# V sums of an attention kernel in four one-bank PSUM tiles, and the last batch's turns split between VectorE and TensorE

## The chip, the cores and the metric

The kernel runs on one NeuronCore of a Trainium2 chip. The metric is the device time of one execution in microseconds. Before the change the median of three runs is 398.49 us (398.30 to 399.39).

## The reference

Two stages follow each other: an attention whose weights are sigmoids, and a soft mixture of experts over all 3584 rows of its output.

```python
# q, k, v: (8 batches, 12 heads, 448 rows, 64)
scores = (q @ k.T) / sqrt(64) - log(448)
attn = 1 / (1 + exp(-scores))
x = heads_side_by_side(attn @ v)          # (8*448, 768)
logits = x @ phi                          # (3584, 32 slots)
d = softmax(logits, axis=0)               # over all rows
slot_input = d.T @ x                      # (32, 768), 4 slots for each of 8 experts
slot_out[e] = relu(slot_input[e] @ w1[e]) @ w2[e]      # 768 -> 1024 -> 768
c = softmax(logits, axis=1)               # over the slots
out = c @ slot_out
```

All of it is float32. The softmax over all rows needs the last batch, so the experts can only start when the attention is over.

## The kernel before

**Attention.** Two heads are a pair; there are 6 pairs in a batch and 48 in all (`NP`). The 448 keys of a pair are three full chunks of 128 (c = 0, 1, 2) and a rest of 64; the rests of an even pair p and of pair p + 1 share one chunk (c = 3). Two pairs thus make seven units: (p,0) (p,1) (p,2) (p,3) (p+1,0) (p+1,1) (p+1,2). There are 21 units in a batch. The loop at L376 takes one unit in each step i: `score` of unit i (four matmuls with 64x64 weights, L146, into an `sc` tile of two PSUM banks, then one sigmoid on ScalarE, L150, into `att`), and `weigh` of unit i - 2 (four matmuls, L175, that add V products into `av`). There are two `sc` tiles.

**The V sums.** `av0` (even pairs) and `av1` (odd pairs) are PSUM tiles of two banks, `[P, 2, 512]`. A chunk's first 64 keys are summed in bank 0 and its last 64 in bank 1 (index t), since the two halves use different rows of the array. After c = 2, `evac_a` (ScalarE, L178) copies bank 1 to `x`; `evac_b` (VectorE, L182) adds bank 0 to it. For an even pair, the unit of the rests stands between the two: its matmuls (called the vl matmuls below, after their operand) add pair p's rest into bank 0 of `av0`, and then write pair p + 1's rest as the first product into bank 1 of `av1`. So `evac_a(p)` reads bank 1 of `av0` while the vl matmuls write bank 0 of the same tile.

```python
o, w = avs[p + t], vls[p // 2][row, r]
start, stop = t == 1, t == 0
nc.tensor.matmul(o[r, t, 0:S], w, att[row, h, :], start=start, stop=stop)
```

**Order.** The engines TensorE, ScalarE, VectorE and the load queue run their instructions in the order in which the code is written. The pool tracks a tile as a whole: a writer waits for the tile's earlier readers. ScalarE's order around a rest is: sigmoid of the unit before, `evac_a`, sigmoid of the rest's own step.

**Between units.** `x` is also needed turned, with rows on the partitions (`y`). VectorE turns it in 32x32 blocks (`turns`, L197); these small instructions wait in the list `todo` and are let out in every step by `work`. Once per batch there are the logits (L215, 24 matmuls), a softmax over them (`softmax_a` on VectorE, `softmax_b` on ScalarE, `softmax_c` on VectorE) and the slot sums (L270, 16 matmuls).

**The last batch.** The logits of its first five pairs (L394) stand behind the scores of the last unit; they are added in `lgt`, an `sc` tile of which VectorE first sets a corner (L390). Pairs 0 to 2 and 3 are turned by VectorE (`turns(0, 0, 3)` and `turns(1, 0, 1)`), pairs 4 and 5 by TensorE transposes against an identity (`turn_pe`, L206) into the two halves of one tile `px`, from which ScalarE (L414, L415, L301) and VectorE (L308, L309) copy them. `warm` (L191) gives TensorE matmuls whose result nobody reads. `last_job` takes the maximum (L294, L296, L298, L303, L305), the exponential (L306), the slot sums (L270) and the turned slot inputs `sT` (L317).

**Experts.** Weights come in units of 384 KB into a ring of 56 + 11 tiles (`wa`, `wb`). The first 56 are loaded during the attention; the 11 `wb` tiles lie where the attention's buffers were and are loaded as these come free. Every further load waits for a ring tile that has been used up; the first of them stands behind the first half of expert 0 (L443). The PSUM pools of this stage (`ps_h` for `ph`, `ps_t` for `pt`, `ps_o` for `po`) take the attention's banks in the order of their lines (L432 to L434). The stage ends with the output's rows, stored through the same load queue.

Of the kernel before, what the change touches and what calls it, by code (L numbers as in the profile page):

```python
# [9 lines left out]
F32 = mybir.dt.float32  # L10
F32R = mybir.dt.float32r
AF = mybir.ActivationFunctionType
ALU = mybir.AluOpType
AX = mybir.AxisListType
PSUM = bass.MemoryType.PSUM

B, H, S, D = 8, 12, 448, 64
DM, NSLOT, E, SPE, F = 768, 32, 8, 4, 1024
P = 128
NFK = 3  # L20
# [14 lines left out]
WN = 128  # L35
CW = 256
NBK = 4
# [11 lines left out]
def soft_moe_attention(ctx: ExitStack, tc: tile.TileContext, qk, v, vl, phi, w1, w2, cst, out):  # L49
    nc = tc.nc  # L50
# [7 lines left out]
    ident = csb[:, 0:128]  # L58
# [6 lines left out]
    acc = small.tile([P, SLN], F32, name="acc")  # L65
# [31 lines left out]
    with ExitStack() as actx:  # L97
# [4 lines left out]
        ps_sc = actx.enter_context(tc.tile_pool(name="ps_sc", bufs=2, space=PSUM))  # L102
        ps_av = actx.enter_context(tc.tile_pool(name="ps_av", bufs=1, space=PSUM))
# [8 lines left out]
        def x_of(p):  # L112
            t, k = divmod(p % NPR, TR)
            return xs[t][:, k, :]
# [38 lines left out]
        def weigh(u):  # L153
            p, c = u
            att = atts.pop(u)
            if c == 0 and p % 2 == 0:
                avs[p] = ps_av.tile([P, 2, 512], F32, name="av0")
            if c == NFK:
                avs[p + 1] = ps_av.tile([P, 2, 512], F32, name="av1")
            if p == NP - 1:  # L160
                for h, r in enumerate(heads):
                    nc.tensor.matmul(
                        avs[p][r, 1, 0:S], vts[p][:, c, r], att[:, h, :], start=False, stop=(c == NFK - 1))
                return
            for t in range(2):
                row = slice(64 * t, 64 * t + 64)
                for h, r in enumerate(heads):
                    if c < NFK:
                        o, w = avs[p], vts[p][row, c, r]
                        start = c == 0 and (p % 2 == 0 or t == 0)  # L170
                        stop = c == NFK - 1 and (p % 2 == 1 or t == 1)
                    else:
                        o, w = avs[p + t], vls[p // 2][row, r]
                        start, stop = t == 1, t == 0
                    nc.tensor.matmul(o[r, t, 0:S], w, att[row, h, :], start=start, stop=stop)  # L175

        def evac_a(p):
            nc.scalar.copy(x_of(p), avs[p][:, 1, 0:S])  # L178

        def evac_b(p):  # L180
            av = avs.pop(p)
            nc.vector.tensor_tensor(out=x_of(p), in0=x_of(p), in1=av[:, 0, 0:S], op=ALU.add)  # L182

        def evac_last(p):
            x, av = x_of(p), avs.pop(p)
            for t in (slice(0, 2 * P), slice(2 * P, S)):
                nc.scalar.copy(x[:, t], av[:, 1, t])

        def warm(pw, n):
            for _ in range(n):  # L190
                nc.tensor.matmul(pw[:, 1, 0:P], ident, ident, start=True, stop=True)  # L191

        def turns(t, k0, n):
            def one(a, g):
# [8 lines left out]
        def turn_pe(px, p):  # L203
            for c in range(NBK):
                n = P if c < NBK - 1 else 64
                nc.tensor.transpose(out=px[0:n, c * P:(c + 1) * P], in_=x_of(p)[:, c * P:c * P + n], identity=ident)  # L206

        def y_of(px, p):
            y = ys[1][:, :, p % TR, :, :].rearrange("p a c k -> p c a k")
            return y, px.rearrange("p (c a k) -> p c a k", c=NBK, a=4)  # L210

        def logits(lg, b, pairs, js=(3, 2, 1, 0)):
            for hp in pairs:
# [71 lines left out]
        def last_job(b, lgt, pw, px):  # L285
            lg = lgt[:, 0, 0:P]
            pa = lgt[:, 1, :]
            old = mz[:, (b - 1) % 2:(b - 1) % 2 + 1]
            t1 = small.tile([P, 2, 132], F32, name="t1")
            pe, zt = t1[:, 0, 0:P], t1[:, 1, 0:P]  # L290
            m1 = small.tile([P, 8], F32, name="m1")
            cw = small.tile([P, 8], F32, name="cw")
            p = b * NPR + NPR - 1
            nc.vector.tensor_reduce(out=m1[:, 0:1], in_=lg, axis=AX.X, op=ALU.max)  # L294
            turn_pe(px[:, 1, :], p)
            nc.tensor.matmul(pa[0:1, 0:P], m1[:, 0:1], ident, start=True, stop=True)  # L296
            mrow = small.tile([1, 1, NSLOT], F32, name="mrow")
            nc.vector.tensor_reduce(  # L298
                out=mrow[:], in_=pa[0:1, 0:P].rearrange("o (j s) -> o s j", j=4), axis=AX.X, op=ALU.max)
            y, yx = y_of(px[:, 1, :], p)  # L300
            nc.scalar.copy(y[:, 0:2], yx[:, 0:2])  # L301
            for j in range(4):
                nc.tensor.matmul(pa[32 * j:32 * j + 32, P:P + 1], mrow[:, 0, :], csb[0:1, 0:1], start=True, stop=True)  # L303
            warm(pw, 2)
            nc.vector.tensor_scalar(cw[:, 0:1], pa[:, P:P + 1], old, -1.0, op0=ALU.max, op1=ALU.mult)  # L305
            nc.scalar.activation(pe, lg, AF.Exp, bias=cw[:, 0:1])  # L306
            nc.scalar.activation(cw[:, 1:2], old, AF.Exp, bias=cw[:, 0:1])
            nc.vector.tensor_copy(y[:, 2], yx[:, 2])  # L308
            nc.vector.tensor_copy(y[0:64, 3], yx[0:64, 3])  # L309
            nc.vector.transpose(zt, pe)  # L310
            warm(pw, 2)
            sl = ps_av.tile([P, 2, 512], F32, name="av1")[:, 0, :]
            slot_mm(sl, zt)
            nc.vector.scalar_tensor_tensor(
                out=acc[:], in0=acc[:], scalar=cw[:, 1:2], in1=sl[:, 0:SLN], op0=ALU.mult, op1=ALU.add)
            sT = small.tile([P, NKC, NSLOT], F32, name="phit")
            nc.vector.transpose(sT[:].rearrange("p k s -> p (k s)"), acc[:])  # L317
            nc.vector.transpose(lt_all[:, b, :], lg)  # L318
            nc.vector.tensor_reduce(out=cw[:, 4:5], in_=pe, axis=AX.X, op=ALU.add)
            nc.vector.scalar_tensor_tensor(  # L320
                out=cw[:, 6:7], in0=mz[:, 2:3], scalar=cw[:, 1:2], in1=cw[:, 4:5], op0=ALU.mult, op1=ALU.add)

            def finish(pool):
                pz = pool.tile([P, 512], F32, name="pt")
                nc.tensor.matmul(pz[:, 0:1], rep, cw[:, 6:7], start=True, stop=True)
                nc.vector.tensor_scalar(rz[:], pz[:, 0:1], 1e-9, None, op0=ALU.add)
                nc.vector.reciprocal(rz[:], rz[:])

            return sT, finish
# [6 lines left out]
        nc.sync.dma_start(phi_sb, phi)  # L336
        nc.sync.dma_start(csb[:], cst)
        load_qk(2)
        pw = ps_av.tile([P, 2, 512], F32, name="av0")
        for _ in range(WARM):  # L340
            nc.tensor.matmul(pw[:, 0, 0:WN], acc[:, 0:P], acc[:, 0:WN], start=True, stop=True)  # L341
        dmy = small.tile([1, 1], F32, name="dmy")
        nc.scalar.activation(dmy[:], nbias[0:1, :], AF.Sigmoid)

# [6 lines left out]
        for b in range(B):  # L351
            u = b * per_b + LAG
            late[u + 10] = [lambda: turns(0, 0, 3)]
            if b < B - 1:
                late[u + 17] = [lambda: turns(1, 0, 2)]
                late[u + 20] = [lambda: turns(1, 2, 1)]
            else:
                late[u + 13] = [lambda: turns(1, 0, 1)]
        for b in range(B - 1):
            u = (b + 1) * per_b + LAG  # L360
            early[u + 1] = [lambda b=b: logits_job(b)]
# [14 lines left out]
        for i in range(len(seq) + LAG):  # L376
# [20 lines left out]
            if i >= LAG:  # L397
                u = seq[i - LAG]
                weigh(u)
                p, c = u  # L400
                if c == NFK:
                    evac_b(p)
                    load_vl(p // 2 + 1)
                elif c == NFK - 1:
                    load_v(p + 2)
                    if p == NP - 1:
                        work(B * S)
                        pw = ps_av.tile([P, 2, 512], F32, name="av0")
                        px = ps_sc.tile([P, 2, 512], F32, name="sc")
                        turn_pe(px[:, 0, :], p - 1)  # L410
                        warm(pw, 2)
                        evac_last(p)
                        y, yx = y_of(px[:, 0, :], p - 1)
                        nc.scalar.copy(y[:, 0:3], yx[:, 0:3])  # L414
                        nc.scalar.copy(y[0:64, 3], yx[0:64, 3])  # L415
                        continue
                    evac_a(p)
                    if p % 2 == 1:
                        evac_b(p)
# [9 lines left out]
    for e in range(E):  # L429
        h = sb2.tile([P, 256], F32, name=f"h{e}", bufs=1)[:]  # L430
        hT.append(h.rearrange("p (f s) -> p f s", f=NFC))
    ps_h = ctx.enter_context(tc.tile_pool(name="ps_h", bufs=2, space=PSUM, reuse_waits="tile"))  # L432
    ps_t = ctx.enter_context(tc.tile_pool(name="ps_t", bufs=4, space=PSUM, reuse_waits="tile"))
    ps_o = ctx.enter_context(tc.tile_pool(name="ps_o", bufs=2, space=PSUM, reuse_waits="tile"))  # L434

    for _ in range(N_B):
# [181 lines left out]
```

## Time and profile before

The profiled execution took 397.56 us, of which 395.8 us are the span of the trace, so 1.76 us lie around it. It is 0.93 us under the median of the three runs.

| | value |
|---|---|
| time of the profiled execution, span | 397.56 us, 395.8 us |
| TensorE matmuls busy | 363.2 us (92%) |
| VectorE busy | 255.7 us (65%) |
| ScalarE busy | 223.2 us (56%) |
| moved by DMA | 95.26 MB, mean 241 GB/s |

The span has two parts: the attention up to about 302 us, in which TensorE is nearly always busy, and the experts with the output behind it, in which the DMA engines are. A share over the whole span tells little of either; each part is read by itself.

In the rows of the timeline the first two numbers are the start and the length in us; then come the engine (PE is TensorE's matmuls, DVE VectorE, ACT ScalarE, SPq the load queue), the line, the operation, what is written and read, and the count. In brackets is the time for which the engine sat idle before it and who ended that. A float32 matmul leaves two records here: four matmuls are "x8".

### The profile page before, as it was taken

The page shows a single profiled execution, that of the slowest core. Times are in us where ns is not written, and L with a number is a line of the kernel's source. Part 1 is how long each engine was busy: PE and PEld are TensorE (multiplying, and loading weights), DVE is VectorE, ACT ScalarE, POOL GpSimd, SP SyncE. Part 2 cuts the span into 40 slices and gives each one's busy share as a digit, 9 for nine tenths or more (in the row PEclk, how much of TensorE's full clock was granted, in tenths as well). Part 3 has the DMA queues.
Part 4 walks back from the last instruction along what each step waited for, and adds up shares of the span by engine and source line. Part 5 has one row for each costly group of instructions (what it writes and reads, how often), then busy time and mean ns, then how long its engine had stood idle before and what let it go on. Part 6 is the DMA issues. An engine that isn't in the chain of part 4 may idle for free.

```text
span 395.8 us, 10094 instructions
## 1 busy us (share of the span) xinstructions
PE 363.2 (92%) x4096; PEld 156.2 (39%) x4096; DVE 255.7 (65%) x688; ACT 223.2 (56%) x308; POOL 3.1 (1%) x14
## 2 busy tenths in 40 slices
PE   8999999999999999999999999999978988999750
PEld 5333444434343434434343444344345643422330
DVE  0158768786888688697868777886944782232450
ACT  5777667676766675675757666756731213422440
POOL 0000000000000000000000000000002000000000
PEclk9999999999999999999999999999989998999985
DMA  6677476656666675665676565433239999999998
GB/s 248 227 234 256 138 253 179 237 199 192 207 228 186 216 235 181 207 231 182 207 233 212 198 206 169 139 119 92 67 130 317 381 400 401 401 400 399 401 409 310
DMA packets 42382, 95.26 MB, mean 241 GB/s; under 512 B 4448, under 2 KB 18528, under 8 KB 42336
## 3 DMA queue, kind: packets, MB, share of 16 engines
q1 hardware_dynamic: 42336, 94.62, 69.0%
q8 instruction: 32, 0.52, 0.5%
q14 instruction: 14, 0.11, 0.1%
HBM read 83.59 MB, written 11.01 MB: 239 GB/s over the span
## 4 chain that ended last, share of the span: by engine, by line
PE 71%; DVE 10%; ACT 8%; DMA 5%; issue 2%; DVEq 0%; ACTq 0%; SPq 0%
PE sc L146 28%; PE av L175 28%; ACT att L150 4%; PE po L545 4%; PE sc L215 3%; DVE y L197 3%; PE sc L270 3%; DMA wa<-in_w_dram 2%; DMA wb<-in_w_dram 2%; ACT x L178 2%; PE pt L489 1%; DMA out_dram<-wa 1%; DVE tmp L458 1%; PE av L341 1%; DVE tmp L457 1%
## 5 line engine op out<-in xcount | busy, mean ns | idle before, releaser
L150 ACT ACTIVATE att<-sc,nbias 128x896 f32<-128x896 f32 x168 | 169.1, 1007 | 94.5 <-PE sc L146 91.8
L146 PE MATMUL sc<-qkt 64*64 64x448 f32 x1344 | 157.2, 538 | 0.4 <-ACT att L150 0.4
L197 DVE STREAM_TRANSPOSE y<-x 32x384 f32<-32x384 f32 (+5 forms) x368 | 148.0, 402 | 5.7
L175 PE MATMUL av<-att,v 64*64 64x448 f32 x1128 | 131.4, 536 | 0.0
L146 PEld LDWEIGHTS sc<-qkt 64*64 64x64 f32 x1344 | 49.8, 133 | 72.5 <-issue 66.1
L175 PEld LDWEIGHTS av<-att,v 64*64 64x64 f32 x1128 | 43.1, 133 | 62.8 <-issue 61.3
L182 DVE TENSOR_TENSOR x<-x,av 128x448 f32<-128x448 f32 x47 | 29.2, 621 | 49.6 <-PE av L175 40.2
L175 PE MATMUL av<-att,vl 64*64 64x448 f32 x192 | 23.2, 554 | 5.6 <-ACT x L178 4.5
L545 PE MATMUL po<-wa,h 128*32 128x384 f32 x224 | 25.6, 519 | 0.0
L178 ACT COPY x<-av 128x448 f32<-128x448 f32 x47 | 24.5, 522 | 0.0
L443 PE MATMUL ph<-wa,phit 128*32 128x256 f32 x336 | 18.5, 379 | 1.3 <-DVE lt_all L318 1.3
L509 DVE COPY wa<-pt 128x384 f32<-128x384 f32 x27 | 13.9, 553 | 8.4 <-PE pt L508 5.0
L509 ACT COPY wa<-ph 128x384 f32<-128x384 f32 x27 | 12.1, 479 | 11.1 <-PE ph L508 8.9
L215 PE MATMUL sc<-x,phit 128*32 128x96 f32 (+1 forms) x384 | 13.3, 274 | 2.2 <-DVE sc L390 2.2
L175 PEld LDWEIGHTS av<-att,vl 64*64 64x64 f32 x192 | 5.7, 132 | 21.9 <-ACT x L178 18.8
L443 PEld LDWEIGHTS ph<-wa,phit 128*32 128x32 f32 x336 | 10.8, 110 | 8.5 <-issue 1.7
L215 PEld LDWEIGHTS sc<-x,phit 128*32 128x32 f32 x384 | 10.7, 115 | 8.1 <-ACT x L178 4.9
L508 PE MATMUL ph<-st,wb 128*128 128x384 f32 x28 | 11.8, 422 | 1.1 <-DVE st L538 1.0
L281 DVE SCALAR_TENSOR_TENSOR acc<-acc,t,sc 128x192 f32<-128x192 f32 x6 | 2.5, 415 | 13.8 <-PE sc L270 13.8
L508 PE MATMUL pt<-st,wb 128*128 128x384 f32 x28 | 9.6, 341 | 1.6 <-DVE st L538 1.6
L460 ACT COPY h<-tmp 128x32 f32<-128x32 f32 x8 | 1.7, 218 | 16.2 <-DVE tmp L458 16.2
L270 PE MATMUL sc<-y,t 128*32 128x192 f32 x224 | 10.6, 329 | 0.0
(98 smaller groups left out, 159.2 us busy)
## 6 DMA issues: line engine op xcount, KB each, us to landing
wa<-in_w_dram SPq DMA_DIRECT2D x112, 384.0 KB, 5.0
qkt<-in_qk_dram SPq DMA_DIRECT2D x48, 448.0 KB, 3.5
out_dram<-wa SPq DMA_DIRECT2D x27, 384.0 KB, 5.6
v<-in_v_dram SPq DMA_DIRECT2D x48, 192.0 KB, 2.5
wb<-in_w_dram SPq DMA_DIRECT2D x16, 384.0 KB, 6.2
vl<-in_vl_dram SPq DMA_DIRECT2D x24, 64.0 KB, 1.9
out_dram<-wb SPq DMA_DIRECT2D x1, 384.0 KB, 7.6
csb<-in_cst_dram SPq DMA_DIRECT2D x1, 128.0 KB, 4.5
```

The lines of the kernel that those rows point to most:

```text
L146: nc.tensor.matmul(sc[64 * t:64 * t + 64, h, 0:S], qkts[pt][r, S + k0:S + k0 + 64], qkts[pt][r, 0:S], start=True, stop=True)
L150: nc.scalar.activation(att[:], sc[:, :, 0:S], AF.Sigmoid, bias=nbias[:], scale=QSCALE)
L175: nc.tensor.matmul(o[r, t, 0:S], w, att[row, h, :], start=start, stop=stop)
L178: nc.scalar.copy(x_of(p), avs[p][:, 1, 0:S])
L182: nc.vector.tensor_tensor(out=x_of(p), in0=x_of(p), in1=av[:, 0, 0:S], op=ALU.add)
L197: nc.vector.transpose(ys[t][32 * g:32 * g + 32, a, k0:k0 + n, 0:nblk(g), :], src)
L215: nc.tensor.matmul(lg[32 * j:32 * j + 32, 0:BLK * nblk(j)], phi_sb[:, hp, :], blocks(x_of(b * NPR + hp), j, nblk(j)), start=(hp == 0), sto ...
L270: nc.tensor.matmul(sl[32 * j:32 * j + 32, 0:SLN], zt[:, c * BLK:(c + 1) * BLK], ys[j // 2][:, a:a + 2, :, c, :], start=(c == 0), stop=(c = ...
L443: nc.tensor.matmul(ph[32 * j:32 * j + 32, 0:256], sT[:, kc, :], utile[("w1", e, j, kc // 3)][:, kc % 3 * 256:(kc % 3 + 1) * 256], start=(k ...
L508: nc.tensor.matmul(pf[:, 0:HALF], ct_of(m), st[:], start=True, stop=True)
L509: (nc.scalar.copy, nc.vector.tensor_copy)[n % 2](ov, pf[:, 0:HALF])
L545: nc.tensor.matmul(po[32 * fl:32 * fl + 32, 0:HALF], hT[e][:, 4 * g + fl, :], ut, start=(n == 0), stop=(n == 2 * E - 1))
```

## The change

- **Four tiles of one bank.** `av0` and `av1` become `av00`, `av01`, `av10`, `av11`, each `[P, 512]`; the index t picks the tile in place of the bank. What is computed, and its order, stays. `pw`, the target of `warm`, and the last slot sums' `sl` become such tiles.
- **Last batch.** `turns(1, 0, 1)` goes: 16 transposes on VectorE. Pair 3 of that batch is turned by TensorE behind the last V products, into the tile `av01`; pairs 4 and 5 go into the two halves of one `sc` tile. Two `warm` matmuls that stood there go. VectorE copies pair 3 to `y`, ScalarE pair 4.
- **Experts.** `ps_t` is made before `ps_h`, so that `ph` lies in banks that `av00` and `av01` had, and `pt` in those of the `sc` tiles.

```diff
             if c == 0 and p % 2 == 0:
-                avs[p] = ps_av.tile([P, 2, 512], F32, name="av0")
+                avs[p] = [ps_av.tile([P, 512], F32, name=f"av0{t}") for t in range(2)]
             if c == NFK:
-                avs[p + 1] = ps_av.tile([P, 2, 512], F32, name="av1")
+                avs[p + 1] = [ps_av.tile([P, 512], F32, name=f"av1{t}") for t in range(2)]
...
-                    nc.tensor.matmul(o[r, t, 0:S], w, att[row, h, :], start=start, stop=stop)
+                    nc.tensor.matmul(o[t][r, 0:S], w, att[row, h, :], start=start, stop=stop)
 
         def evac_a(p):
-            nc.scalar.copy(x_of(p), avs[p][:, 1, 0:S])
+            nc.scalar.copy(x_of(p), avs[p][1][:, 0:S])
...
-            turn_pe(px[:, 1, :], p)
+            turn_pe(px[2], p)
...
             if b < B - 1:
                 late[u + 17] = [lambda: turns(1, 0, 2)]
                 late[u + 20] = [lambda: turns(1, 2, 1)]
-            else:
-                late[u + 13] = [lambda: turns(1, 0, 1)]
...
-                        pw = ps_av.tile([P, 2, 512], F32, name="av0")
-                        px = ps_sc.tile([P, 2, 512], F32, name="sc")
-                        turn_pe(px[:, 0, :], p - 1)
-                        warm(pw, 2)
+                        pw = ps_av.tile([P, 512], F32, name="av00")
+                        px = [ps_av.tile([P, 512], F32, name="av01")]
+                        pxs = ps_sc.tile([P, 2, 512], F32, name="sc")
+                        px += [pxs[:, t, :] for t in range(2)]
+                        for t in range(2):
+                            turn_pe(px[t], p - 2 + t)
                         evac_last(p)
-                        y, yx = y_of(px[:, 0, :], p - 1)
-                        nc.scalar.copy(y[:, 0:3], yx[:, 0:3])
-                        nc.scalar.copy(y[0:64, 3], yx[0:64, 3])
+                        for t, copy in enumerate((nc.vector.tensor_copy, nc.scalar.copy)):
+                            y, yx = y_of(px[t], p - 2 + t)
+                            copy(y[:, 0:3], yx[:, 0:3])
+                            copy(y[0:64, 3], yx[0:64, 3])
                         continue
...
+    ps_t = ctx.enter_context(tc.tile_pool(name="ps_t", bufs=4, space=PSUM, reuse_waits="tile"))
     ps_h = ctx.enter_context(tc.tile_pool(name="ps_h", bufs=2, space=PSUM, reuse_waits="tile"))
-    ps_t = ctx.enter_context(tc.tile_pool(name="ps_t", bufs=4, space=PSUM, reuse_waits="tile"))
```

Three places show what moves on the engines. The first is TensorE around the rests of one pair of pairs. Before, `av_247` is the even pair's tile and `av_288` the odd pair's; a name with `_49` is a semaphore of the engine or of a load queue.

```order
L146 MATMUL sc<-qkt 64x448 [waits Activation_49]
L146 MATMUL sc<-qkt 64x448 x3
L175 MATMUL av_247<-att,vl 64x448 [waits DMAHW4_49,Activation_49]
L175 MATMUL av_247<-att,vl 64x448
L175 MATMUL av_288<-att,vl 64x448 [waits DVE_49]
L175 MATMUL av_288<-att,vl 64x448
L146 MATMUL sc<-qkt 64x448 [waits PE_49]
```

The same place of the changed kernel: `av_249` is the even pair's bank 0, `av_292` and `av_291` are the odd pair's bank 1 and bank 0.

```order
L146 MATMUL sc<-qkt 64x448 [waits Activation_49]
L146 MATMUL sc<-qkt 64x448 x3
L175 MATMUL av_249<-att,vl 64x448 [waits DMAHW4_49]
L175 MATMUL av_249<-att,vl 64x448
L175 MATMUL av_292<-att,vl 64x448 x2
L146 MATMUL sc<-qkt 64x448 [waits Activation_49]
L146 MATMUL sc<-qkt 64x448 x3
L175 MATMUL av_291<-att,v_236 64x448 [waits DMAHW7_49,DVE_49]
```

The first vl matmul no longer waits for ScalarE, only for its load. The wait for VectorE has moved from the third vl matmul to the next V products; a wait for ScalarE now stands at the next scores.

The second place is VectorE at the end of the last batch, first before (`y_95` and `x_93` hold pairs 0 to 2, `y_96` and `x_94` pairs 3 to 5).

```order
L197 STREAM_TRANSPOSE y_95<-x_93 32x3x96 x7
L197 STREAM_TRANSPOSE y_96<-x_94 32x128 [waits DVE_49]
L197 STREAM_TRANSPOSE y_96<-x_94 32x128 x7
L182 TENSOR_TENSOR x_94<-x_94,av_3215 128x448 [waits PE_49,Activation_49]
L197 STREAM_TRANSPOSE y_96<-x_94 32x96 x5
L390 MEMSET sc 64x32 [waits Activation_49]
L197 STREAM_TRANSPOSE y_96<-x_94 32x96 x3
L294 TENSOR_REDUCE m_3330<-sc 128x1 [waits DVE_49,PE_49]
```

And in the changed kernel, where the memset has become L388:

```order
L197 STREAM_TRANSPOSE y_95<-x_93 32x3x96 x7
L182 TENSOR_TENSOR x_94<-x_94,av_3261 128x448 [waits PE_49,Activation_49]
L388 MEMSET sc 64x32 [waits Activation_49]
L415 COPY y_96<-av_3346 128x3x4x32 [waits PE_49]
L416 COPY y_96<-av_3346 64x4x32
L294 TENSOR_REDUCE m_3367<-sc 128x1 [waits DVE_49,PE_49]
```

The 16 transposes are gone, 13 of them from ahead of the memset; two copies stand ahead of the maximum.

The third place is TensorE behind the last V products, first before (L206 are the transposes, L191 is `warm`).

```order
L206 MATMUL sc<-csb,x_94 128x128 [waits PE_49]
L206 MATMUL sc<-csb,x_94 128x128 x2
L206 MATMUL sc<-csb,x_94 64x128
L191 MATMUL av_3313<-csb 128x128 x2
L215 MATMUL sc<-x_94,phit 32x128 [waits Activation_49]
L215 MATMUL sc<-x_94,phit 32x128
L215 MATMUL sc<-x_94,phit 32x96 x2
L206 MATMUL sc<-csb,x_94 128x128 [waits Activation_49]
```

And in the changed kernel, where `av_3346` is pair 3's target:

```order
L206 MATMUL av_3346<-csb,x_94 128x128 x3
L206 MATMUL av_3346<-csb,x_94 64x128
L206 MATMUL sc<-csb,x_94 128x128 [waits PE_49]
L206 MATMUL sc<-csb,x_94 128x128 x2
L206 MATMUL sc<-csb,x_94 64x128
L215 MATMUL sc<-x_94,phit 32x128 [waits Activation_49]
L215 MATMUL sc<-x_94,phit 32x128
L215 MATMUL sc<-x_94,phit 32x96 x2
L206 MATMUL sc<-csb,x_94 128x128 [waits Activation_49]
```

Four transposes stand where two `warm` matmuls were; the transposes of the last pair still wait for ScalarE's copy out of the other half of their tile.

More of the change, by code (lines that the diff above doesn't have):

```diff
@@ L162, in weigh @@
                     nc.tensor.matmul(
-                        avs[p][r, 1, 0:S], vts[p][:, c, r], att[:, h, :], start=False, stop=(c == NFK - 1))
+                        avs[p][1][r, 0:S], vts[p][:, c, r], att[:, h, :], start=False, stop=(c == NFK - 1))
                 return
@@ L174, in weigh @@
                         start, stop = t == 1, t == 0
-                    nc.tensor.matmul(o[r, t, 0:S], w, att[row, h, :], start=start, stop=stop)
+                    nc.tensor.matmul(o[t][r, 0:S], w, att[row, h, :], start=start, stop=stop)
         def evac_a(p):
-            nc.scalar.copy(x_of(p), avs[p][:, 1, 0:S])
+            nc.scalar.copy(x_of(p), avs[p][1][:, 0:S])
         def evac_b(p):
             av = avs.pop(p)
-            nc.vector.tensor_tensor(out=x_of(p), in0=x_of(p), in1=av[:, 0, 0:S], op=ALU.add)
+            nc.vector.tensor_tensor(out=x_of(p), in0=x_of(p), in1=av[0][:, 0:S], op=ALU.add)
         def evac_last(p):
@@ L186, in evac_last @@
             for t in (slice(0, 2 * P), slice(2 * P, S)):
-                nc.scalar.copy(x[:, t], av[:, 1, t])
+                nc.scalar.copy(x[:, t], av[1][:, t])
         def warm(pw, n):
             for _ in range(n):
-                nc.tensor.matmul(pw[:, 1, 0:P], ident, ident, start=True, stop=True)
+                nc.tensor.matmul(pw[:, 0:P], ident, ident, start=True, stop=True)
         def turns(t, k0, n):
@@ L209, in y_of @@
             y = ys[1][:, :, p % TR, :, :].rearrange("p a c k -> p c a k")
-            return y, px.rearrange("p (c a k) -> p c a k", c=NBK, a=4)
+            return y, px[:, 0:NBK * P].rearrange("p (c a k) -> p c a k", c=NBK, a=4)
         def logits(lg, b, pairs, js=(3, 2, 1, 0)):
@@ L299, in last_job @@
                 out=mrow[:], in_=pa[0:1, 0:P].rearrange("o (j s) -> o s j", j=4), axis=AX.X, op=ALU.max)
-            y, yx = y_of(px[:, 1, :], p)
+            y, yx = y_of(px[2], p)
             nc.scalar.copy(y[:, 0:2], yx[:, 0:2])
@@ L311, in last_job @@
             warm(pw, 2)
-            sl = ps_av.tile([P, 2, 512], F32, name="av1")[:, 0, :]
+            sl = ps_av.tile([P, 512], F32, name="av10")
             slot_mm(sl, zt)
@@ L338, in soft_moe_attention @@
         load_qk(2)
-        pw = ps_av.tile([P, 2, 512], F32, name="av0")
+        pw = ps_av.tile([P, 512], F32, name="av00")
         for _ in range(WARM):
-            nc.tensor.matmul(pw[:, 0, 0:WN], acc[:, 0:P], acc[:, 0:WN], start=True, stop=True)
+            nc.tensor.matmul(pw[:, 0:WN], acc[:, 0:P], acc[:, 0:WN], start=True, stop=True)
         dmy = small.tile([1, 1], F32, name="dmy")
@@ L407, in soft_moe_attention @@
                         work(B * S)
-                        pw = ps_av.tile([P, 2, 512], F32, name="av0")
-                        px = ps_sc.tile([P, 2, 512], F32, name="sc")
-                        turn_pe(px[:, 0, :], p - 1)
-                        warm(pw, 2)
+                        pw = ps_av.tile([P, 512], F32, name="av00")
+                        px = [ps_av.tile([P, 512], F32, name="av01")]
[3 more added lines that the diff above has]
+                            turn_pe(px[t], p - 2 + t)
                         evac_last(p)
-                        y, yx = y_of(px[:, 0, :], p - 1)
-                        nc.scalar.copy(y[:, 0:3], yx[:, 0:3])
-                        nc.scalar.copy(y[0:64, 3], yx[0:64, 3])
+                        for t, copy in enumerate((nc.vector.tensor_copy, nc.scalar.copy)):
+                            y, yx = y_of(px[t], p - 2 + t)
+                            copy(y[:, 0:3], yx[:, 0:3])
+                            copy(y[0:64, 3], yx[0:64, 3])
                         continue
```

## The prediction

> **What bounds the kernel now.** I read the page first, then the busy time by stage, the waits, and the timeline where the waits stand. All durations come from the profiled execution: 397.56 us, its span 395.8 us.
>
> ```profile
> span 395.8 us, 10094 instructions
> 102.00:138.00 36.00, 35.25 (x424) 14.63 (x419) 28.26 (x76) 24.10 (x30) 0.00 (x0) 1.00 0.61 203
> 310.00:320.00 10.00, 10.00 (x192) 6.01 (x188) 7.85 (x30) 2.11 (x8) 0.00 (x0) 1.00 1.03 404
> 303.63 26.68 SPq L91 DMA_DIRECT2D wa<-in_w_dram  x30
> ```
>
> The stage rows give the stretch, its length, then the busy time of PE, PEld, DVE, ACT and POOL, the granted clock, the DMA share and GB/s. In one batch of the attention TensorE is busy 35.25 of 36 us, VectorE 28.26, ScalarE 24.10: TensorE is the bound, and only its own pauses can be won. In the experts the DMA engines are full (share 1.03, 404 GB/s). The loads of that part start at 303.63, when the first ring tiles have been used up, and a fixed amount follows. So what counts is **how much earlier 303.63 comes**; whatever is won before it moves the whole end, and nothing after it matters.
>
> ```profile
> PEld av L175 <- ACT x L178: 18.8, 17, 1.4
> PE av L175 <- ACT x L178: 4.5, 7, 0.6
> ```
>
> These rows of the waits (total us, times, longest) say that the V products waited 17 times for `evac_a`, 7 of them so long that the matmuls themselves stood idle. There are 24 units of rests, one for each two pairs. The timeline shows the three kinds: 10 quiet ones, 7 at a batch's boundary, 7 behind the slot sums.
>
> **Part 1, the four tiles.** A quiet one:
>
> ```profile
> 104.87 0.93 PE L146 MATMUL sc<-qkt 64*64 64x448 f32 x8
> 105.33 0.52 ACT L178 COPY x<-av 128x448 f32<-128x448 f32 x1
> 105.91 0.21 PEld L175 LDWEIGHTS av<-att,vl 64*64 64x64 f32 x8 [0.88 <-ACT x L178]
> 105.93 1.01 ACT L150 ACTIVATE att<-sc,nbias 128x896 f32<-128x896 f32 x1
> 106.71 0.93 PE L146 MATMUL sc<-qkt 64*64 64x448 f32 x8
> 107.64 0.75 PE av L175 x8
> ```
>
> The chain (last row) shows 0.75 us from one group of four matmuls to the next when nothing waits. Here the scores start at 104.87 and the vl matmuls at 105.91, 1.04 later; the next scores come 0.80 behind them. That is 1.84 instead of 1.50: **0.34 us**. ScalarE's copy ends at 105.85, and the vl matmuls follow at once, though they write the other bank.
>
> At a batch's boundary the copy stands behind `softmax_b`:
>
> ```profile
> 117.34 0.93 PE L146 MATMUL sc<-qkt 64*64 64x448 f32 x8
> 118.13 0.31 ACT L249 ACTIVATE t<-t 128x129 f32<-128x129 f32 x1
> 118.35 0.51 ACT L178 COPY x<-av 128x448 f32<-128x448 f32 x1
> 118.76 1.01 ACT L150 ACTIVATE att<-sc,nbias 128x896 f32<-128x896 f32 x1
> 118.92 0.98 PE L175 MATMUL av<-att,vl 64*64 64x448 f32 x8 [0.65 <-ACT x L178]
> 119.72 0.93 PE L146 MATMUL sc<-qkt 64*64 64x448 f32 x8
> 154.91 0.98 PE L175 MATMUL av<-att,vl 64*64 64x448 f32 x8 [0.65 <-ACT x L178]
> ```
>
> Scores to vl 1.58, to the next scores 0.80: 2.38 instead of 1.50, **0.88 us**. The next batch's is at 154.91, 36.0 us on. Behind the slot sums nothing is lost, as TensorE comes late by itself.
>
> The changed order has no wait for ScalarE at the vl matmuls, so this removes 10 x 0.34 + 7 x 0.88 = **9.56 us**, if nothing else is late next. What is next: the scores two steps on need the `sc` tile that the sigmoid of this step reads. In the quiet case the vl matmuls would start at 105.62 and those scores 2.25 later, at 107.87; the sigmoid ends at 106.94, 0.93 to spare. At the boundary they come at 117.34 + 3.00 = 120.34, the sigmoid ends at 119.77: 0.57 to spare. ScalarE itself does not move, since its copy and its sigmoid stay in order. VectorE's `evac_b` waits for the vl matmuls and comes earlier with them; the wait for the previous `evac_b` moves one group later. The loads need 0.61 of the DMA engines over a batch; 1.22 us less per batch makes that 0.63. I cost all these at nothing.
>
> **Part 2, the last batch.** All rows of its end, with two of the clock:
>
> ```profile
> 282.55 5.91 DVE L197 STREAM_TRANSPOSE y<-x 32x288 f32<-32x288 f32 x15
> 287.53 0.97 PE L162 MATMUL av<-att,v 128*64 128x448 f32 x4
> 288.47 0.62 DVE L182 TENSOR_TENSOR x<-x,av 128x448 f32<-128x448 f32 x1
> 289.11 1.41 DVE L197 STREAM_TRANSPOSE y<-x 32x96 f32<-32x96 f32 x5
> 290.53 0.09 DVE L390 MEMSET sc<- 64x32 f32 x1
> 290.00:295.00 5.00, 4.33 (x48) 2.46 (x48) 1.40 (x6) 0.23 (x2) 0.00 (x0) 0.66 0.45 170
> 290.67 2.29 PE L215 MATMUL sc<-x,phit 128*32 128x96 f32 x40 [2.17 <-DVE sc L390]
> 292.89 2.36 PE L162 MATMUL av<-att,v 128*64 128x448 f32 x8
> 295.00:300.00 5.00, 4.54 (x58) 3.35 (x60) 1.49 (x6) 2.13 (x7) 0.57 (x2) 1.00 0.74 227
> 295.18 0.66 PE L206 MATMUL sc<-csb,x 128*128 128x128 f32 x4
> 295.68 0.61 PE L191 MATMUL av<-csb 128*128 128x128 f32 x4
> 295.88 0.48 ACT L414 COPY y<-sc 128x384 f32<-128x384 f32 x1
> 296.25 0.26 ACT L415 COPY y<-sc 64x128 f32<-64x128 f32 x1
> 296.56 0.66 PE L206 MATMUL sc<-csb,x 128*128 128x128 f32 x4
> 301.43 0.38 DVE L317 STREAM_TRANSPOSE phit<-acc 128x192 f32<-128x192 f32 x1
> 301.73 0.27 DVE L318 STREAM_TRANSPOSE lt_all<-sc 128x128 f32<-128x128 f32 x1
> 302.15 1.50 PE L443 MATMUL ph<-wa,phit 128*32 128x256 f32 x24 [1.32 <-DVE lt_all L318]
> 112.83 1.52 PE L215 MATMUL sc<-x,phit 128*32 128x96 f32 x48
> ```
>
> - **The wait of 2.17 us goes.** The logits wait for the memset, which stands behind `evac_b` of pair 4 and 13 transposes of pair 3. Without these VectorE is through its earlier list by 282.55 + 7 x 0.47 = 285.84. `evac_b` then waits only for the vl matmuls (about 1.1 us behind their start, so 287.0 here), and the memset is done by 287.8, before TensorE wants the logits at 288.5.
> - **The slow clock goes.** Behind that pause the granted clock is 0.66 in the mean of 290 to 295, which is half clock for 5.0 x 0.34 / 0.5 = 3.4 us, and 1.00 again after. At full clock 48 records of the logits take 1.52, so 40 take 1.27 instead of 2.29: 1.02. The eight of L162 take 2.29 from start to start; four of 0.97 with a tail of some 0.17 give 1.60 for eight: 0.69. Together 1.71.
> - **The turns cost something.** The four added transposes (0.50 to the next start) stand in for two `warm` matmuls (0.53): nothing. But pair 4's now come second, so ScalarE's copy starts 0.50 later, and pair 5's transposes, which wait for it (296.56), too. The maximum's matmuls are queued behind those, and the whole chain to L443 follows: -0.50. VectorE's two copies end about when the logits do (0.72 behind the transposes' start, then 0.55 and 0.27, nearest row the copy below): nothing, up to 0.1.
> - **The other banks.** L443 starts 0.15 behind the end of L318 (302.00), which reads the bank that `ph` takes. In the changed pools `ph` waits only for L317 (301.81): 0.19.
>
> ```profile
> L509 DVE COPY wa<-pt 128x384 f32<-128x384 f32 x27 | 13.9, 553 | 8.4 <-PE pt L508 5.0
> 298.07 1.16 PE L191 MATMUL av<-csb 128*128 128x128 f32 x8
> 299.32 1.51 PE L270 MATMUL av<-y,t 128*32 128x192 f32 x32
> ```
>
> Sum of part 2: 2.17 + 1.71 - 0.50 + 0.19 = **3.57 us**.
>
> [...] If the drop had another cause than this pause and stayed, the sum would be 1.71 less.
>
> **Sum.** 9.56 + 3.57 = 13.1 us, all ahead of 303.63, with the DMA-bound rest unchanged: 397.56 - 13.1 = 384.4 for an execution like the profiled one. The median of the runs stands 0.93 above it (398.49), and I keep that offset: **385.4 us**.
>
> **The rivals.**
>
> *The half clock comes back behind the turns* (13%). The transposes might not count as work for the clock. When it fell, TensorE had worked 0.97 us (L162) of the 3.1 us before 290.67. In the changed kernel, from the first transposes on, 1.5 us of transposes, a pause of 0.5 and two short waits for VectorE leave about as little ordinary work. Price: L191 and L270 behind it at half clock, 1.16 + 1.51 = 2.7 us, so 388.1. Against it: the same place before, with eight transposes and one `warm` group, has 1.00 in the row of 295 to 300. [...]
>
> *ScalarE becomes the wait* (8%). If the sigmoid at a boundary is later than the 0.57 to spare, because VectorE's softmax ahead of `softmax_b` shifts, the 7 gains of 0.88 are given back: 6.2 us, 391.6. For it: ScalarE runs copy and two sigmoids without a pause there. Against it: the chain of that softmax starts from TensorE's own logits and shifts with them.
>
> *The vl matmuls wait as before* (3%), through a wait that the order doesn't make plain, such as the new one for ScalarE at the next scores reaching the copy: only part 2 remains, 394.9. Against: that wait is for a sigmoid, ahead of the copy in ScalarE's queue.
>
> *Slower* (4%): TensorE's pauses may be what keeps its clock. With 36.0 of 36 us busy, the granted clock could fall over the whole attention. Against: it is 1.00 with 35.25 busy. To lose the 13.1 us and 1.2 more, the 287 us up to the last logits would have to grow by 5%, a mean clock under 0.95; at 0.93 the time would be near 407.
>
> **Range and chances.** 70% for the forecast, with 383.5 to 387 as its own range: 384.4 is the profiled base, the offset of the median may be anything from 0 to 1.8 (the highest run), and the half-clock term may be missing (+1.7). The first rival reaches 388.1, with the same offset spread 389. That is 383.5 to 389.0 for 8 in 10. A measurement here tells about 0.3%, 1.2 us, from no change. Faster: 0.70 + 0.13 + 0.08 + 0.03 = 0.94; slower 0.04; the same 0.02, for what I overlooked.
>
> **What would show it.** Right: no wait of L175 for L178 is left, scores to vl takes 0.75 to 0.80 in all 24 places, and a batch takes 34.8 us instead of 36.0. The memset stands before the logits want it, the granted clock stays at 1.00 from 288 to 303 of the old count, pair 5's transposes start 0.5 us later behind the last V products, and the first late load is issued near 290.5. Wrong: idle time of the scores (L146) that ends with a sigmoid, a clock of 0.50 behind the transposes, or an expert part longer than the 92 us from 303.63 to the span's end, which would say that the loads, not the attention, carry the time.

## The result and the profile after

The changed kernel takes 386.06 us (median of four runs, 385.45 to 387.07) against 398.86 us before (four runs): ratio 0.9682, 95% interval 0.9653 to 0.9710. The forecast was 385.4 us. The profiled execution took 385.61 us, 1.8 us of them outside its span. Three executions of 622 to 623 us with a granted clock of 0.56, and one of 2065 us, stand in no ratio and no trace of this document.

The page's first line, the vl matmuls' group (count, then busy time and mean ns, then idle time before it), the same group before the change, and one stretch of 35 us in the middle of the attention (length, then busy time of PE, PEld, DVE, ACT and POOL, granted clock, DMA share, GB/s; PEld is TensorE's weight loads):

```profile
span 383.8 us, 10063 instructions
...
L175 PE MATMUL av<-att,vl 64*64 64x448 f32 x192 | 22.4, 536 | 0.0
```

```profile
L175 PE MATMUL av<-att,vl 64*64 64x448 f32 x192 | 23.2, 554 | 5.6 <-ACT x L178 4.5
```

```profile
93.00:128.00 35.00, 35.00 (x424) 14.99 (x420) 28.25 (x75) 24.11 (x29) 0.00 (x0) 1.00 0.67 218
```

TensorE now has no pause in the attention behind its start (busy 267.00 of the 267.00 us from 10 to 277), and its clock stays at 1.00. TensorE sat idle for 5.6 us ahead of vl matmuls before, now never. The start of the late loads has come from 303.63 to this row of the load queue:

```profile
291.47 38.36 SPq L91 DMA_DIRECT2D wa<-in_w_dram  x42
```

From there to the span's end it is 92.3 us, against 92.2 before: the expert part is as long as it was, within what it differs from trace to trace (last section).

A batch's boundary in the timeline of the changed kernel, at the place where 0.88 us were lost:

```profile
114.96 0.93 PE L146 MATMUL sc<-qkt 64*64 64x448 f32 x8
115.42 0.30 ACT L248 ACTIVATE t<-t 128x129 f32<-128x129 f32 x1
115.71 0.93 PE L175 MATMUL av<-att,vl 64*64 64x448 f32 x8
115.76 0.31 ACT L249 ACTIVATE t<-t 128x129 f32<-128x129 f32 x1
115.97 0.52 ACT L178 COPY x<-av 128x448 f32<-128x448 f32 x1
116.39 2.09 ACT L150 ACTIVATE att<-sc,nbias 128x896 f32<-128x896 f32 x2
116.46 0.93 PE L146 MATMUL sc<-qkt 64*64 64x448 f32 x8
```

The vl matmuls start 0.75 behind the scores and before ScalarE's copy has even begun; the next scores follow 0.75 later. ScalarE does the same things in the same order. Its copy out of one bank takes 0.52 us as before, and the matmuls that write the other bank meanwhile take 0.93, as the scores around them do: here neither is slower for the other's work. In all 24 places scores to vl is now 0.75 to 0.80, and a batch takes 34.8 us instead of 36.0.

The end of the attention, in the timeline and in two rows of the clock:

```profile
277.46 0.93 PE L175 MATMUL av<-att,vl 64*64 64x448 f32 x8
278.50 0.62 DVE L182 TENSOR_TENSOR x<-x,av 128x448 f32<-128x448 f32 x1 [0.72 <-PE av L175]
279.08 0.97 PE L162 MATMUL av<-att,v 128*64 128x448 f32 x4
279.13 0.09 DVE L388 MEMSET sc<- 64x32 f32 x1
279.98 1.30 PE L215 MATMUL sc<-x,phit 128*32 128x96 f32 x40
281.21 1.72 PE L162 MATMUL av<-att,v 128*64 128x448 f32 x8
282.86 0.66 PE L206 MATMUL av<-csb,x 128*128 128x128 f32 x4
283.36 0.60 PE L206 MATMUL sc<-csb,x 128*128 128x128 f32 x4
283.89 0.41 PE L215 MATMUL sc<-x,phit 128*32 128x128 f32 x8
284.37 0.26 ACT L416 COPY y<-sc 64x128 f32<-64x128 f32 x1
284.68 0.66 PE L206 MATMUL sc<-csb,x 128*128 128x128 f32 x4 [0.38 <-ACT y L416]
287.34 1.51 PE L270 MATMUL av<-y,t 128*32 128x192 f32 x32
289.46 0.38 DVE L317 STREAM_TRANSPOSE phit<-acc 128x192 f32<-128x192 f32 x1
289.98 1.50 PE L444 MATMUL ph<-wa,phit 128*32 128x256 f32 x24 [1.14 <-DVE phit L317]
```

```profile
280.00:285.00 5.00, 4.62 (x69) 2.80 (x68) 1.04 (x3) 2.99 (x7) 0.00 (x0) 1.00 0.79 253
285.00:290.00 5.00, 3.49 (x57) 2.25 (x55) 2.15 (x9) 0.92 (x3) 1.67 (x7) 1.00 0.99 336
```

The memset is done at 279.22, before the logits (279.98) want it. They and the V products of the last pair behind them (L162) run at full clock. Pair 5's transposes (284.68) wait 0.38 us for ScalarE's copy of pair 4, and the first expert matmuls follow the end of L317 (289.84) by 0.14.

Three stretches carry the comparison from here on: **first to last vl matmul**, **last vl matmul to first expert matmul**, and from there to the span's end.

| us | before | after |
|---|---|---|
| start to first vl matmul | 12.21 | 12.98 |
| first to last vl matmul | 273.65 | 264.48 |
| last vl matmul to first expert matmul | 16.29 | 12.52 |
| first expert matmul to the span's end | 93.6 | 93.8 |

### The profile page after: what moved, and what is told of

Same layout as the page of the kernel before. It is cut to its first block, busy times and chain, and to the rows that moved or that the text cites. A ratio compares the mean times of both kernels' runs of the same rounds, so it can differ in the third digit from the quotient of the medians.

```text
span 383.8 us, 10063 instructions
## 1 busy us (share of the span) xinstructions
PE 359.8 (94%) x4096; PEld 158.6 (41%) x4096; DVE 252.2 (66%) x674; ACT 223.7 (58%) x308; POOL 3.1 (1%) x14
## 3 DMA queue, kind: packets, MB, share of 16 engines
HBM read 83.59 MB, written 11.01 MB: 246 GB/s over the span
## 4 chain that ended last, share of the span: by engine, by line
PE 82%; DVE 7%; DMA 4%; ACT 2%; issue 1%; DVEq 0%; ACTq 0%; SPq 0%
PE sc L146 34%; PE av L175 32%; PE po L546 4%; PE sc L215 3%; PE sc L270 3%; DMA wa<-in_w_dram 2%; DMA wb<-in_w_dram 2%; PE pt L490 2%; PE av L341 1%; DVE tmp L459 1%; DVE wa L510 1%; DVE tmp L458 1%; PE ph L509 1%; PE pt L509 1%; PE av L162 1%
## 5 line engine op out<-in xcount | busy, mean ns | idle before, releaser
L197 DVE STREAM_TRANSPOSE y<-x 32x384 f32<-32x384 f32 (+5 forms) x352 | 143.4, 407 | 5.5
L175 PE MATMUL av<-att,v 64*64 64x448 f32 x1128 | 131.4, 536 | 0.0
L175 PEld LDWEIGHTS av<-att,v 64*64 64x64 f32 x1128 | 43.1, 133 | 62.8 <-issue 61.3
L175 PE MATMUL av<-att,vl 64*64 64x448 f32 x192 | 22.4, 536 | 0.0
L509 PE MATMUL ph<-st,wb 128*128 128x384 f32 x28 | 12.6, 450 | 1.0 <-DVE st L539 1.0
L215 PEld LDWEIGHTS sc<-x,phit 128*32 128x32 f32 x384 | 9.9, 110 | 5.8 <-ACT x L178 4.9
L215 PE MATMUL sc<-x,phit 128*32 128x96 f32 (+1 forms) x384 | 12.3, 262 | 0.0
L509 PE MATMUL pt<-st,wb 128*128 128x384 f32 x28 | 10.5, 374 | 1.6 <-DVE st L539 1.6
L175 PEld LDWEIGHTS av<-att,vl 64*64 64x64 f32 x192 | 7.3, 133 | 10.7 <-issue 10.7
L270 PE MATMUL sc<-y,t 128*32 128x192 f32 x224 | 10.6, 329 | 0.0
```

The lines of the kernel that those rows point to most:

```text
L175: nc.tensor.matmul(o[t][r, 0:S], w, att[row, h, :], start=start, stop=stop)
L197: nc.vector.transpose(ys[t][32 * g:32 * g + 32, a, k0:k0 + n, 0:nblk(g), :], src)
L215: nc.tensor.matmul(lg[32 * j:32 * j + 32, 0:BLK * nblk(j)], phi_sb[:, hp, :], blocks(x_of(b * NPR + hp), j, nblk(j)), start=(hp == 0), sto ...
L270: nc.tensor.matmul(sl[32 * j:32 * j + 32, 0:SLN], zt[:, c * BLK:(c + 1) * BLK], ys[j // 2][:, a:a + 2, :, c, :], start=(c == 0), stop=(c = ...
L509: nc.tensor.matmul(pf[:, 0:HALF], ct_of(m), st[:], start=True, stop=True)
```

## The experiments

The theory: 9.2 us come from the waits of the vl matmuls for a copy out of the other bank of their tile, and some 3.6 us from the end of the last batch, where a memset behind a list of transposes stalled TensorE and cost it its clock. The main rivals: the gain comes from one part alone, the half clock has another cause, the moved transposes cost clock themselves.

**The tiles alone** (`av0` and `av1` split as in the change; last batch and pools as before):

```diff
-                avs[p] = ps_av.tile([P, 2, 512], F32, name="av0")
+                avs[p] = [ps_av.tile([P, 512], F32, name=f"av0{t}") for t in range(2)]
...
-                    nc.tensor.matmul(o[r, t, 0:S], w, att[row, h, :], start=start, stop=stop)
+                    nc.tensor.matmul(o[t][r, 0:S], w, att[row, h, :], start=start, stop=stop)
```

> The four one-bank tiles alone, on the kernel before. Theory: they take away the 17 waits of the vl matmuls and nothing else. From the first vl matmul to the last 264.5 us as with the whole change (273.65 before); from the last vl matmul to the first expert matmul 16.6 us (16.29 before: VectorE's list does not move, so TensorE waits the 0.34 us won at the last vl matmul longer for the memset, 2.5 instead of 2.17 us, and the half clock stays). Time 9.2 us under the kernel before, ratio 0.977. Rival, that the tiles also shorten the end of the attention: the second stretch near 12.5 and the ratio 0.968.

Ratio 0.9779 (0.9761 to 0.9796), 8.8 us. First to last vl matmul 264.49; last vl matmul to first expert matmul 16.25. The end of the attention in its timeline, and the row of the clock:

```profile
278.42 0.97 PE L162 MATMUL av<-att,v 128*64 128x448 f32 x4
279.70 0.62 DVE L182 TENSOR_TENSOR x<-x,av 128x448 f32<-128x448 f32 x1
280.34 1.40 DVE L197 STREAM_TRANSPOSE y<-x 32x96 f32<-32x96 f32 x5
281.76 0.09 DVE L390 MEMSET sc<- 64x32 f32 x1
281.90 2.36 PE L215 MATMUL sc<-x,phit 128*32 128x96 f32 x40 [2.51 <-DVE sc L390]
284.19 2.06 PE L162 MATMUL av<-att,v 128*64 128x448 f32 x8
286.18 0.66 PE L206 MATMUL sc<-csb,x 128*128 128x128 f32 x4
```

```profile
280.00:285.00 5.00, 3.10 (x44) 2.19 (x46) 2.58 (x10) 1.13 (x2) 0.00 (x0) 0.66 0.58 228
```

The first stretch has the whole gain. In the second TensorE comes 0.34 us earlier and waits that much longer (2.51 instead of 2.17), and the half clock is there too. The stretch was 0.3 shorter than expected, for two reasons. The clock fell at 281.50, 0.40 us before the wait ended, so that logits and V products lost less (from start to start 4.28 us for both instead of 4.51). And the slot sums came 4.04 us behind the first transposes instead of 4.13: written to a tile of one bank, they start 0.06 instead of 0.15 behind VectorE's last turn ahead of them (L310). The odd tile alone gives the same (4.05 us, in the run of that name below); why, no run shows. Apart from these 0.09 us the tiles do nothing for the end.

**The last batch alone** (`turns(1, 0, 1)` dropped, pair 3 turned by TensorE into bank 1 of the even tile; tiles and pools as before):

```diff
-            else:
-                late[u + 13] = [lambda: turns(1, 0, 1)]
...
+                        px = [pw[:, 1, :]]
+                        pxs = ps_sc.tile([P, 2, 512], F32, name="sc")
+                        px += [pxs[:, t, :] for t in range(2)]
+                        for t in range(2):
+                            turn_pe(px[t], p - 2 + t)
```

> The last batch's part alone: two-bank V tiles, order of the expert pools as before, pair 3 turned by TensorE into one bank of the even V tile. Theory: first vl matmul to last 273.65 us as before; last vl matmul to first expert matmul 12.8 us instead of 16.29, with no wait for the memset and the clock at 1.00. Time 3.5 us under the kernel before, ratio 0.991. Rival, that the half clock is not from the pause: the wait goes but the clock row still shows 0.50, the stretch is near 14.4 and the ratio 0.995.

Ratio 0.9915 (0.9889 to 0.9941), 3.4 us. The trace comes from one more run of the same kernel:

> The last batch's part alone once more, for its trace. Theory: first vl matmul to last 273.65 us with the 17 waits for the copy; then no wait of the logits for the memset, clock 1.00, and 12.8 us from the last vl matmul to the first expert matmul. Rival, that the half clock is not from the pause: the logits take more than 1.4 us and the stretch is over 13.5.

First to last vl matmul 273.65, last vl matmul to first expert matmul 12.85. Its waits (total, times, longest), and its timeline:

```profile
PEld av L175 <- ACT x L178: 18.8, 17, 1.4
PE av L175 <- ACT x L178: 4.5, 7, 0.6
```

```profile
287.86 0.09 DVE L388 MEMSET sc<- 64x32 f32 x1
...
288.71 1.30 PE L215 MATMUL sc<-x,phit 128*32 128x96 f32 x40
...
289.94 1.72 PE L162 MATMUL av<-att,v 128*64 128x448 f32 x8
```

All 17 waits of the vl matmuls are there to the tenth of a microsecond; the wait for the memset and the slow logits (2.29 us) are gone. The two parts are independent: 12.85 less the 0.20 for the pools' order (below), the 0.05 that the last vl matmul still loses and the 0.09 of the slot sums' tile is 12.51, against 12.52 of the whole.

**Only the odd tile split** (the even pair's stays one tile of two banks):

```diff
-                avs[p] = ps_av.tile([P, 2, 512], F32, name="av0")
+                av = ps_av.tile([P, 2, 512], F32, name="av0")
+                avs[p] = [av[:, t, :] for t in range(2)]
```

> Only the odd pair's V tile is split in two; the even pair's stays one tile of two banks. Theory: the wait that counts is that of the vl matmuls for ScalarE's copy out of the even tile's other bank, so nothing changes: first vl matmul to last 273.65 us, 17 waits for the copy, ratio 1.000 within 0.003. Rival, that the wait for VectorE at the third vl matmul (which this takes away, since the odd tile's bank 0 is now written one group later) was part of the gain: some of the 9.2 us appear here, ratio under 0.997.

Ratio 0.9997 (0.9980 to 1.0014); first to last vl matmul 273.65. Its waits and its timeline at the end (its lines stand one lower, so L176 here is L175 elsewhere):

```profile
PEld av L176 <- ACT x L179: 18.8, 17, 1.4
```

```profile
291.13 1.73 PE L216 MATMUL sc<-x,phit 128*32 128x96 f32 x40 [2.17 <-DVE sc L391]
292.79 2.93 PE L163 MATMUL av<-att,v 128*64 128x448 f32 x8
```

All 17 waits for the copy are there, so the moved wait for VectorE is worth nothing; the gain is in the even tile, whose bank 1 is being copied. The pause is 2.17 us as before, but the slow part fell on the V products (2.93) rather than the logits (1.73): the half clock starts 0.72 us behind the pause instead of 0.13 (last section).

**The pools' order put back** (in the changed kernel):

```diff
-    ps_t = ctx.enter_context(tc.tile_pool(name="ps_t", bufs=4, space=PSUM, reuse_waits="tile"))
     ps_h = ctx.enter_context(tc.tile_pool(name="ps_h", bufs=2, space=PSUM, reuse_waits="tile"))
+    ps_t = ctx.enter_context(tc.tile_pool(name="ps_t", bufs=4, space=PSUM, reuse_waits="tile"))
```

> The changed kernel with the order of the expert pools put back, so that the first expert sums take the bank that the last logits are read from. Theory: the first expert matmul starts 0.14 us behind the end of the turn of the logits (L318) instead of behind that of the slot inputs (L317): last vl matmul to first expert matmul 12.7 us instead of 12.52. Not to be told in the time: ratio 0.968 to 0.969 as with the whole change. Rival, that the banks matter to the whole expert stage: more than 0.5 us between the first late load and the end.

Last vl matmul to first expert matmul 12.72 us, 0.20 more; ratio 0.9679 (0.9657 to 0.9700). The order of the pools is worth 0.2 us in the trace and cannot be told in the time. From the first late load to the span's end it took 92.9 us against 92.3, so the rival's sign of over 0.5 us came by the number. But the other kernels have 92.1 to 93.5 there with either order, so this trace does not tell the banks' effect on the expert part from that spread.

**Two versions of the end.** Beside the changed kernel again, the first keeps VectorE's turns of pair 3 but lets them out behind the memset (tiles and pools as changed, TensorE's part as before the change); the second gives pair 5's turned rows a tile of their own.

```diff
-                late[u + 13] = [lambda: turns(1, 0, 1)]
+                late[u + 18] = [lambda: turns(1, 0, 1)]
```

```diff
-                        px += [pxs[:, t, :] for t in range(2)]
+                        px += [pxs[:, 0, :]]
...
                         evac_last(p)
+                        px.append(ps_av.tile([P, 512], F32, name="av11"))
```

> The changed kernel once more, to stand beside the next two on the same chip: ratio 0.968, last vl matmul to first expert matmul 12.52 us.

> The four tiles and the changed order of the pools, but pair 3 turned by VectorE as before, with its 16 transposes let out behind the memset instead of ahead of it; the turns on TensorE and the warm matmuls as before. Theory: what cost was the place of the memset, not the turns. The memset comes before TensorE wants the logits, clock 1.00, the 16 transposes (4.5 us) end before the maximum is wanted, and pair 5's transposes start 1.38 us behind pair 4's as in the kernel before instead of 1.82: last vl matmul to first expert matmul 12.1 to 12.2 us, 0.35 to 0.44 us better than the change, ratio 0.967. Rival, that VectorE has too much to do there: the maximum (L294) waits for the transposes and the stretch is over 12.6.

> The changed kernel with a tile of its own (the free odd V tile) for pair 5's turned rows. Theory: pair 5's transposes then no longer wait for ScalarE's copy of pair 4 out of the other half of the tile; they start right behind the last logits, 1.38 us instead of 1.82 behind the first transposes, and the chain to the experts is 0.3 to 0.44 us shorter: last vl matmul to first expert matmul 12.1 to 12.2 us, ratio 0.967. Rival, that VectorE's two copies of pair 3 ahead of the maximum hold the chain instead: the transposes start earlier but the maximum's matmul (L296) does not, and the stretch stays at 12.5.

The changed kernel: 0.9670 (0.9649 to 0.9690); its stretch stays the 12.52 us of the first trace. Turns behind the memset: 0.9658 (0.9640 to 0.9676), last vl matmul to first expert matmul 12.09 us. Own tile: 0.9663 (0.9644 to 0.9682), 12.06 us. First the timeline of the version with the turns behind the memset, then that of the one with its own tile:

```profile
279.19 0.09 DVE L390 MEMSET sc<- 64x32 f32 x1
...
279.48 4.47 DVE L197 STREAM_TRANSPOSE y<-x 32x128 f32<-32x128 f32 x15
280.04 1.30 PE L215 MATMUL sc<-x,phit 128*32 128x96 f32 x40
...
284.30 0.66 PE L206 MATMUL sc<-csb,x 128*128 128x128 f32 x4
284.45 0.29 DVE L294 TENSOR_REDUCE m<-sc 128x1 f32<-128x128 f32 x1 [0.51 <-PE sc L215]
```

```profile
282.81 0.41 PE L215 MATMUL sc<-x,phit 128*32 128x128 f32 x8
283.15 0.65 PE L206 MATMUL av<-csb,x 128*128 128x128 f32 x4
283.30 0.29 DVE L294 TENSOR_REDUCE m<-sc 128x1 f32<-128x128 f32 x1
283.74 0.38 PE L296 MATMUL sc<-csb,m 128*1 128x128 f32 x2
```

In the first the 16 transposes end at 283.95, 0.5 us before the maximum wants VectorE. It was the place of the memset that cost, not the turns; moving them to TensorE was not needed. In the second pair 5's transposes follow the logits at once. Each version has 0.43 to 0.46 us less in the stretch than the change, about as worked out. In the time that is at most shown as a tendency, since the three intervals overlap.

**Transposes and the clock.** In the changed kernel 64 more transposes, or 30 ordinary matmuls with the identity, behind the turns; nothing of the result depends on them. Against the theory that transposes hold the clock stands the first rival of the prediction, that they do not; by both, the ordinary matmuls hold it.

```diff
+                        for _ in range(16):
+                            turn_pe(px[1], p - 1)
```

```diff
+                        warm(pw, 30)
```

> The changed kernel with 64 more TensorE transposes (pair 4 turned 16 more times into the same place) behind the turns, ahead of the last logits: some 8 us in which TensorE does nothing but transposes. Theory: transposes keep the clock: the granted clock stays at 1.00 through them and behind them, four take 0.50 us, and the time is 8 us above that of the change, near 394. [...]

> The same with 30 ordinary matmuls against the identity (60 records of about 0.13 us) in place of the 64 transposes. Both theories: clock 1.00 throughout, 8 us above the change, near 394. It is the control for the run with transposes.

One execution each: 391.59 and 392.23 us; last vl matmul to first expert matmul 19.51 and 18.78. The transposes in the timeline of the first, and two stretches of it:

```profile
282.59 7.59 PE L206 MATMUL sc<-csb,x 128*128 128x128 f32 x68
```

```profile
282.00:286.00 4.00, 4.00 (x38) 3.91 (x37) 0.75 (x2) 0.60 (x2) 0.00 (x0) 1.00 0.89 299
286.00:290.00 4.00, 4.00 (x39) 3.91 (x36) 0.00 (x0) 0.00 (x0) 0.00 (x0) 1.00 0.79 288
```

The clock is 1.00 through 7.5 us of nothing but transposes, and the matmuls behind them are as fast as with the ordinary matmuls (L191 1.16 us, L270 1.51 in both). So 7.59 us of float32 transposes did not lower the clock here. The size was missed: one after another they take 0.11 us, not 0.125, so the stretch grew by 7.0 us, not by 8, and by 6.3 with the ordinary matmuls.

## Why the prediction was right, point by point

- **What bounds.** The gain had to come ahead of the late loads and would then move the whole end: the loads moved by 12.2 us, the span by 12.0, and the expert part kept its length.
- **The four tiles, 9.56 us.** First to last vl matmul leaves out the 0.29 before the first and the 0.05 behind the last: 9.22 expected there, 9.17 measured, and 9.16 with the tiles alone. That the cause is the copy out of the other bank of the even tile is shown by exclusion: the odd tile alone leaves all 17 waits for it, both tiles together leave none. The even tile alone was not run.
- **The covers held.** The sigmoid had 0.57 us to spare at a boundary. In the changed kernel the waits name only one group of scores whose matmuls wait for a sigmoid, the second of all at 7.67 us, and that one was there before. The weight loads ahead of scores name the sigmoid nine times (2.9 us, once before), so some are now close; but the matmuls stood idle for none of the other eight. ScalarE did not become the wait.
- **The end, 3.57 us.** Measured 3.72 (16.29 less 12.52, less the 0.05 that belongs to the last vl matmul). The pause: L162 to the logits took 3.14 and takes 0.90, 2.24 for 2.17. The clock: the logits and the V products take 1.23 and 1.65 instead of 2.22 and 2.29, 1.63 for 1.71. The turns: pair 5's transposes come 1.82 us behind the first instead of 1.38, and the slot sums 4.48 instead of 4.04 (the version with the turns behind the memset, same tiles), so 0.44 for 0.50. VectorE's two copies cost nothing, as put: the maximum starts 0.49 us behind the start of the last logits with and without them. The pools: 0.19, as put. Not in the sum: the 0.09 that the slot sums' one-bank tile gave.
- **The half clock behind the turns** (13%) did not come. The row at 1.00 (280 to 290) and the run with 64 transposes (1.00 from 282 to 290) rule it out for this kernel.
- **The pause as the cause of the half clock** was measured, not only argued: the kernels with a pause of 2.17 or 2.51 us (before, tiles alone, odd tile) have it, at 0.50, those without don't: the last batch alone has 1.00 from 285 to 300 us, and with the turns behind the memset the logits take 1.30 us, as they do in the changed kernel at 1.00. A pause of 2.17 us was followed by it in two traces (before, odd tile).
- **What was not in the sum.** The profiled execution of the changed kernel lost 1.06 us at its start (first vl matmul at 12.98, where 11.92 was to be expected). That is 12.0 in the spans, where 13.1 was worked out. The expert part was 0.2 longer. So 384.4 for the profiled execution missed by 1.2. The offset of 0.93 us that was kept for the median came out smaller, 0.45 (386.06 less 385.61), and so the forecast of 385.4 missed by 0.7 only. That these two misses went against each other is luck; the two sums, 9.56 and 3.57, did not need it.

## What to carry to other kernels

The waits that the pool puts in go by tile, not by bank (17 with the even tile of two banks, none with both tiles split): where one engine copies out of one half of a PSUM tile and TensorE writes the other, two tiles of one bank take the wait away, here at no cost. Look for it where a matmul group starts right at the end of a copy that it has no data from. And a short instruction that TensorE waits for (a memset of a corner) has to stand ahead of an engine's background work, since the pause can cost twice: once itself (2.17 us here), and once in the clock behind it (1.63).

## What was unexpected of the hardware

- **The half clock's place.** After the same pause of 2.17 us it hit the logits in one kernel (2.29 and 2.36 us for logits and V products) and mostly the V products in another (1.73 and 2.93). The granted clock in the traces is 0.50 from 290.80 to 294.21 us before, from 291.85 to 295.26 with the odd tile alone and from 281.50 to 284.91 with the tiles alone: 3.41 us each time (worked out from rows of 0.5 us; the one from 290.50 shows 0.80, so 0.20 us of it are at half clock). It began 0.13 and 0.72 us behind the pause of 2.17 us, and with the tiles alone 0.40 ahead of the end of a pause of 2.51. The trace before has two more drops, at 328.35 and 382.96, 37.55 and 92.16 us behind the first; the trace after has three, at 316.95, 361.32 and 371.56, the later two 44.37 and 54.61 us behind the first. Divided by 3.41, these four distances give 11.01, 27.03, 13.01 and 16.01. What sets the places is not shown.
- **TensorE's work ahead of a drop.** In the 3.41 us just ahead of the three drops above TensorE was busy for 1.24, 1.24 and 1.30 us. Ahead of the other drops it was 0.34 and 1.65 us in the trace before and 1.10, 1.79 and 1.98 in the one after. The trace before also has 3.41 us with 1.84 us of work (369.31 to 372.72) that the clock of 1.00 followed. So the busy time alone does not tell when the clock drops, and it is not shown that every execution of the kernel before has the half clock at this place.
- **The start.** The same first instructions take different times in different executions: the first scores (16 records) 1.73 us in the profile before and 2.46 in the one after, and the first vl matmul starts between 11.90 and 13.04 us in the kernels with split tiles. This spread is larger than the effects of the last two versions.
- **The expert part** differs by 1.4 us between traces (93.6 to 95.0 from the first expert matmul to the span's end) for the same loads, which also hides them.
